# Block 0 of a fused attention forward and backward: hand-written PE and DVE lists in place of the unrolled ones

## The chip, the cores and the metric

One core of one Trainium2 chip. The metric is the device time of one execution in microseconds (us). TensorE is called PE, VectorE DVE, ScalarE ACT, GpSimd POOL, and SP is the engine that issues most DMAs.

## The reference: what is computed

A transformer block and the gradients of its input and its weights, for a sequence of 2048 rows of width 512 in bf16:

```
xn  = layernorm(x)
s   = attention(xn)            # 32 heads of 16 columns, softmax over 2048 keys, then @ wo
g   = silu(mlp(layernorm(xn))) # 512 -> 1792 -> 512, gelu
out = x + s * g
grads = vjp(out)(grad_out)     # for x, wqkv, wo, w1, b1, w2, b2
```

For each head the attention needs the scores q.k, their exponentials, and for the gradients the products dO.v, multiplied by the exponentials, in both orientations: with keys as rows (for what is summed over keys) and with queries as rows (for what is summed over queries).

## The kernel before, in words

The kernel has three stages: `phase_pre` (projections, the MLP forward; 0 to 208 us of the profile), `attention_core` (208 to 1980 us) and `phase3` (the remaining gradients). The change lies in `attention_core`.

**Blocks and steps.** Heads are taken in 16 pairs. A block is one pair and one quarter of the queries (512 of them), so there are 64 blocks; each has 16 steps, one for each 128 keys. Steps are numbered through, g = 0 to 1023; block 0 is g = 0 to 15. A step is made of units, each with a letter:

- `s` (PE, line 806): scores of 128 keys by 512 queries for both heads; two matmuls. `S` (ACT, line 834): the exponential, `et`.
- `d0`, `d1` (PE, line 828): the dO.v products of one head each, one matmul each, and `m0`, `m1` (DVE, line 845): their products with `et`, written to `gts`. Every second step SP turns a pair of steps of `gts` by a DMA transpose into `gk` (line 854).
- `a1` (PE, lines 865 and 868) and `a2` (line 878): sums over keys, from `et` and from `gts`, into one PSUM tile `X` that lasts a block. At the end of a block DVE copies X (`xs`), PE turns it (`XT`), DVE copies that (`xt`), and DVE and POOL make the rows' weights W1 and W2 from it (`sm`, lines 898 to 929).
- The q-major units belong to the block before: `t` (PE, line 818) and its exponential `T` (ACT, line 839), or, for 3 of the 16, a turned copy of `et`: `E` (PE transposes, line 790) and `eE` (DVE, line 795). Then `ze` and `zg` (PE, lines 938 and 946) sum over queries into `Z`, and `acc` (DVE, line 961) adds it up.

**The order.** PE, DVE and ACT run hand-written lists. `PE_ORDER` (line 691) and `DVE_ORDER` (line 699) hold one block's order, as unit and step; `unrolled` (line 976) repeats them for all blocks and drops what does not exist. A loop (line 1034) emits from the three lists in turn, as soon as what a unit needs has been emitted; on the chip each engine runs its list in order, and semaphores do the waiting. SP and POOL have no lists: a scheduler places their instructions.

In block 0 there is no block before it, so `t`, `T`, `ze`, `zg` and `acc` are dropped, and PE's list starts like this:

```
s:0 d1:0 s:1 d0:0 d1:1 s:2 d0:1 d1:2 a1:0 s:3 d0:2 d1:3 s:4 a1:1 a1:2 d0:3 a2:0 a2:1 a2:2 s:5 d1:4 d0:4 s:6 ...
```

and ends `... d1:13 s:14 d0:13 a1:11 d1:14 a2:11 s:15 d0:14 a1:12 a2:12 d1:15 E:11 s:16`. Here something else is put in, right behind each `s` from g = 2 on (line 1047): first the four pieces of `tail` that `phase_pre` left over (two sets of PE transposes of the last rows, line 311, and the two last projections `do_proj(14)` and `do_proj(15)`, line 324; each is followed by an ACT copy, lines 315 and 325, and DMAs), and from g = 6 to 15 two extra matmuls by `emit_warm` (line 1021), whose result nobody reads. That makes 20 of them.

**Buffers.** `s` and `t` share two PSUM tiles, so `s` of step g + 2 waits for `S` of step g. `d0` and `d1` have one PSUM bank each, so d0 of step g + 1 waits until m0 of step g has read it. `Z`, `ET`, `XT`, the `tail` pieces and the extra matmul (`warm`) take turns in one bank, the pool `ps_z`. There are 8 `et`, 4 `gts` (two steps each) and 6 `gk` tiles.

**PE's tiling.** `s` and `d` use 32 rows of the array each, so two matmuls of `s` and both of `d` can run side by side; `a1`, `a2`, `ze` and `zg` use all rows and 32 or 17 columns, so that four run side by side; `E` and the extra matmul use the whole array.

Of the kernel before, what the change touches and what calls it, by code (L numbers as in the profile page):

```python
# [690 lines left out]
PE_ORDER = """  # L691
# [7 lines left out]
DVE_ORDER = """  # L699
# [16 lines left out]
def attention_core(ctx, tc, opnds, ps_z, tail, NAT_s, NATQ_s, Oall, dQall, dKVT_out, ident_f32, ident_bf, npairs=16, nqc=4, turned=(0, 1, 2)):  # L716
# [124 lines left out]
    def emit_mult(g, hj):  # L841
        if g // 2 not in st_gts:
            st_gts[g // 2] = gtp.tile([128, 2, 2, 512], bf16, name="gts")
        gts = st_gts[g // 2]
        nc.vector.tensor_tensor(out=gts[:, g % 2, hj], in0=st_d.pop((g, hj))[:], in1=st_et[g][:, hj], op=ALU.mult)  # L845

    def emit_dmat(g):
        j, kb = divmod(g, 16)
        kc = kb // 4
        kbp = (kb // 2) % 2  # L850
        if kbp == 0:
            blk[j].setdefault("Gk", {})[kc] = gbp.tile([128, 2, 16, 128], bf16, name="gk")
        gk = blk[j]["Gk"][kc]
        nc.sync.dma_start_transpose(out=gk[:, kbp], in_=st_gts[g // 2][:].rearrange("k a h q -> k (a h q)"))
# [26 lines left out]
    def emit_xs(j):  # L881
        xs = xsp.tile([128, 512], f32, name="xs")
        nc.vector.tensor_copy(out=xs[:], in_=blk[j].pop("X")[:])
        blk[j]["xs"] = xs
# [8 lines left out]
    def emit_xt(j):  # L893
        xt = finp.tile([128, 4, 128], f32, name="xt")
        nc.vector.tensor_copy(out=xt[:], in_=blk[j].pop("XT")[:])
        blk[j]["xt"] = xt

    def emit_finish(j):
        p, qc = blocks[j]
        NQq = cur_op[p]["NATQq"]  # L900
        NQd = cur_op[p]["NATQd"]
        xt = blk[j].pop("xt")
        XTv = xt[:].rearrange("q b (r c) -> q b r c", r=4)
        W1 = wp.tile([128, 4, 2, 32], bf16, name="W1")
        W2 = wp.tile([128, 4, 2, 32], bf16, name="W2")
        nc.gpsimd.memset(W2[:, :, :, 0:16], 0.0)
        st0 = qc * 4
        nqs = NQq[:, st0:st0 + 4, :, 1:17]
        ndo = NQd[:, st0:st0 + 4, :, :]
        rL = finp.tile([128, 4, 2, 1], f32, name="rL")  # L910
        nc.vector.reciprocal(out=rL[:], in_=XTv[:, :, 2:4, 17:18])  # L911
        nc.gpsimd.tensor_tensor(out=W1[:, :, :, 0:16], in0=ndo, in1=rL[:].to_broadcast([128, 4, 2, 16]), op=ALU.mult)  # L912
        dl = finp.tile([128, 4, 2, 1], f32, name="dl")
        nc.vector.tensor_tensor(out=dl[:], in0=XTv[:, :, 2:4, 0:1], in1=rL[:], op=ALU.mult)
        ndr = finp.tile([128, 4, 2, 1], f32, name="ndr")
        nc.vector.scalar_tensor_tensor(out=ndr[:], in0=dl[:], scalar=-1.0, in1=rL[:], op0=ALU.mult, op1=ALU.mult)
        nc.gpsimd.tensor_tensor(out=W1[:, :, :, 16:32], in0=nqs, in1=ndr[:].to_broadcast([128, 4, 2, 16]), op=ALU.mult)
        nc.gpsimd.tensor_tensor(out=W2[:, :, :, 16:32], in0=nqs, in1=rL[:].to_broadcast([128, 4, 2, 16]), op=ALU.mult)
        Ov = Oall[:, st0:st0 + 4, p * 32:(p + 1) * 32].rearrange("q b (h c) -> q b h c", h=2)
        nc.gpsimd.tensor_tensor(out=Ov, in0=XTv[:, :, 0:2, 16:32], in1=rL[:].to_broadcast([128, 4, 2, 16]), op=ALU.mult)  # L920
        t1 = finp.tile([128, 4, 2, 16], f32, name="t1")
        nc.gpsimd.tensor_tensor(out=t1[:], in0=XTv[:, :, 0:2, 0:16], in1=dl[:].to_broadcast([128, 4, 2, 16]), op=ALU.mult)
        nc.gpsimd.tensor_tensor(out=t1[:], in0=XTv[:, :, 2:4, 1:17], in1=t1[:], op=ALU.subtract)
        rL4 = finp.tile([128, 4, 2, 1], f32, name="rL4")
        nc.gpsimd.tensor_scalar(out=rL4[:], in0=rL[:], scalar1=0.25, scalar2=None, op0=ALU.mult)
        dQv = dQall[:, st0:st0 + 4, p * 32:(p + 1) * 32].rearrange("q b (h c) -> q b h c", h=2)
        nc.gpsimd.tensor_tensor(out=dQv, in0=t1[:], in1=rL4[:].to_broadcast([128, 4, 2, 16]), op=ALU.mult)
        blk[j]["W1"] = W1
        blk[j]["W2"] = W2
# [43 lines left out]
    def turned_step(g):  # L973
        return g % 16 % 4 == 3 and g % 16 // 4 in turned

    def unrolled(order):
        items = [x.split(":") for x in order.split()]
        items = [(k, int(r)) for k, r in items]
        late = ("t", "T", "ze", "zg", "acc")
        return [(k, 16 * b + r) for b in range(-2, NB + 3) for k, r in items  # L980
                if (16 if k in late else 0) <= 16 * b + r < (NSTEP + 16 if k in late else NSTEP)]

    pe = unrolled(PE_ORDER)
    dve = unrolled(DVE_ORDER)
    act = []
    for g in range(NSTEP + 16):
        if g < NSTEP:
# [7 lines left out]
    issued = set()  # L995

    def needs(k, g):
        if k in ("s", "t"):
            i = place[("S" if k == "s" else "T", g)]
            return [act[i - 2]] if i >= 2 else []  # L1000
        if k in ("d0", "d1"):
            return [("m" + k[1], g - 1)] if g else []
        if k == "a1":
            return [("S", g)] + ([("xs", g - 1)] if g % 16 == 0 and g else [])
        if k == "a2":
            return [("m0", g), ("m1", g), ("a1", g - g % 16)]
        if k == "ze":
            e = ("eE", g - 16) if turned_step(g) else ("T", g)
            return [e, ("sm", g - g % 16 - 1)] + ([before[k, g]] if (k, g) in before else [])
        if k in ("E", "XT"):  # L1010
            return [("S", g) if k == "E" else ("xs", g)] + ([before[k, g]] if (k, g) in before else [])
        if k == "S":
            return [("s", g)]
        if k == "T":
            return [("t", g)]
        if k in ("m0", "m1"):
            return [("S", g), ("d" + k[1], g)]
        return {"acc": [("zg", g)], "xs": [("a1", g), ("a2", g)], "xt": [("XT", g)], "sm": [("xt", g)],
                "eE": [("E", g)], "zg": [("ze", g)]}[k]

    def emit_warm():

        w = ps_z.tile([128, 512], f32, name="warm", tag="z")
        nc.tensor.matmul(w[:], lhsT=cur_op[0]["KVT"][:, 0:128], rhs=cur_op[0]["KVT"][:, 0:512], start=True, stop=True)

    act_of = {"s": emit_s, "t": emit_t, "d0": lambda g: emit_d(g, 0), "d1": lambda g: emit_d(g, 1), "a1": emit_a1, "a2": emit_a2,
              "ze": emit_ze, "zg": emit_zg, "XT": lambda g: emit_XT(g // 16), "E": emit_E, "S": emit_exp_a, "T": emit_exp_b,
              "m0": lambda g: emit_mult(g, 0), "m1": lambda g: emit_mult(g, 1), "acc": emit_acc, "xs": lambda g: emit_xs(g // 16),
              "xt": lambda g: emit_xt(g // 16), "sm": lambda g: emit_finish(g // 16), "eE": emit_eE}
    ET_ = mybir.EngineType  # L1030
    with tc.manual_schedule(engines={ET_.PE, ET_.Activation, ET_.DVE}):
        lists = [act, dve, pe]
        at = [0, 0, 0]
        while any(a < len(l) for a, l in zip(at, lists)):
            moved = False
            for n, l in enumerate(lists):
                while at[n] < len(l) and all(x in issued for x in needs(*l[at[n]])):
                    k, g = l[at[n]]
                    act_of[k](g)
                    issued.add((k, g))  # L1040
                    at[n] += 1
                    moved = True
                    if k in ("m0", "m1") and g % 2 == 1 and ("m0", g) in issued and ("m1", g) in issued:
                        emit_dmat(g)
                    if k == "s":
                        j, kb = divmod(g, 16)
                        if tail and g >= 2:
                            tail.pop(0)()
                        elif 2 <= g < 16:
                            emit_warm()  # L1050
                            emit_warm()
                        p, qc = blocks[j]
                        if kb == 2 and qc == min(1, nqc - 1) and p + 1 < npairs:
                            load_pair(p + 1)
                        if g % 3 == 0 and load_q:
                            load_q.pop(0)()
                    if n == 2:
                        break
            assert moved, [l[a] for a, l in zip(at, lists) if a < len(l)]
# [116 lines left out]
```

## Time and profile before

| | us |
|---|---|
| median of 3 runs | 2370.25 (2368.81 to 2373.88) |
| the profiled execution | 2366.34 |
| its span, first to last instruction | 2364.3 |
| PE, ACT, DVE busy in the span | 2246.3, 2044.5, 2027.1 |
| first `s` of block 0 (step 0) | 208.15 |
| first `s` of block 1 (step 16) | 245.40 |
| last `s` (step 1023) | 1957.3 |

The profile's times count from the first instruction. A line of the timeline gives start, length, engine, source line, operation, tiles written and read, and how many were merged; in brackets stands the engine's idle time before it and what ended it. A line of the table by stretch gives, for each engine, the busy time and the number of instructions, then the TensorE clock that was granted (1.00 is full), the share of time in which the 16 DMA engines were busy, and what they moved. Consecutive `s` are 2.33 us apart in block 0 on average (37.25 us for 16 steps) and 1.70 us in the rest (1711.9 us for 1007 steps).

### The profile page before, as it was taken

To read this page: it belongs to the slowest core of one execution; us is meant where nothing else is said; L and a number is where in the kernel's file an instruction comes from. 1 tells how busy PE (TensorE), PEld (TensorE's weight loads), DVE (VectorE), ACT (ScalarE), POOL (GpSimd) and SP (SyncE) were. 2 spreads that over 40 slices of the span, in tenths; PEclk is the share of its full clock that TensorE was granted. 3 is DMA by queue.
4 is the path that set the end of the run, shared out by engine and by line. 5 is a ranking of instruction groups with operands and counts; after the bars stand their busy time and mean duration, and the time that the engine had idled before them with its cause. 6 is when DMAs were issued, how large, how long until landed. Compare 5 with 4: busy or idle time off the path is not lost.

```text
span 2364.3 us, 51036 instructions
## 1 busy us (share of the span) xinstructions
PE 2246.3 (95%) x20148; PEld 799.7 (34%) x20148; DVE 2027.1 (86%) x3600; ACT 2044.5 (86%) x2336; POOL 313.2 (13%) x753
## 2 busy tenths in 40 slices
PE   7897999999999999999999999999999998889698
PEld 3332333333333333333333333333333333334343
DVE  7566899999999999999999999999999996776164
ACT  6564899999999999999999999999999998783143
POOL 4221011111111111111111111111111112100000
PEclk9998999999999999999999999999999999999899
DMA  9877899999999999999999999999999997786961
GB/s 254 257 227 183 154 165 179 170 169 180 165 182 164 186 163 177 168 178 169 172 178 167 177 165 188 161 181 167 177 167 177 157 158 200 201 206 125 193 160 63
DMA packets 1349730, 415.56 MB, mean 176 GB/s; under 512 B 1272689, under 2 KB 1337586, under 8 KB 1349490
## 3 DMA queue, kind: packets, MB, share of 16 engines
q1 hardware_dynamic: 1346306, 403.66, 90.7%
q0 software_dynamic: 1600, 5.24, 0.6%
q8 instruction: 157, 2.57, 0.4%
q10 hardware_dynamic: 1584, 3.41, 0.4%
q14 instruction: 83, 0.68, 0.1%
HBM read 46.52 MB, written 49.03 MB: 40 GB/s over the span
## 4 chain that ended last, share of the span: by engine, by line
PE 74%; DVE 8%; issue 2%; ACT 2%; DMA 2%; SPq 1%; POOL 0%; ACTq 0%; DVEq 0%; POOLq 0%
PE d L828 12%; PE X L865 11%; PE s L806 11%; PE Z L946 9%; PE X L878 7%; PE Z L938 5%; DVE gts L845 5%; PE t L818 4%; PE ET L790 4%; PE XT L890 2%; PE ps_dw L574 1%; PE X L868 1%; PE ps_dy L629 1%; PE ps_dwkv L677 1%; PE ps_dhg L589 1%
## 5 line engine op out<-in xcount | busy, mean ns | idle before, releaser
L845 DVE TENSOR_TENSOR gts<-d,et 128x512 bf16<-128x512 f32 x2048 | 1321.7, 684 | 79.8 <-PE d L828 23.7
L834 ACT ACTIVATE et<-s 128x1024 bf16<-128x1024 f32 x1024 | 1043.6, 1044 | 15.1 <-PE s L806 12.9
L839 ACT ACTIVATE e<-t 128x1024 bf16<-128x1024 f32 x832 | 866.8, 1043 | 21.5 <-PE t L818 4.1
L828 PE MATMUL d<-QDT,KVT 32*128 32x512 bf16 x2048 | 759.7, 383 | 16.6 <-DVE gts L845 15.3
L806 PE MATMUL s<-QDT,KVT 32*128 32x512 bf16 x2048 | 398.0, 384 | 1.6 <-ACT et L834 1.1
L946 PE MATMUL Z<-gk,W 128*32 128x512 bf16 x2048 | 397.1, 384 | 0.0
L865 PE MATMUL X<-et,Lc 128*32 128x512 bf16 x2048 | 368.7, 388 | 0.0
L868 PE MATMUL X<-et,NAT 128*32 128x512 bf16 x2048 | 367.4, 387 | 0.0
L878 PE MATMUL X<-gts,NAT 128*17 128x512 bf16 x2048 | 329.4, 381 | 0.0
L818 PE MATMUL t<-KVT,QDT 32*128 32x512 bf16 x1664 | 323.2, 383 | 1.0 <-ACT e L839 1.0
L938 PE MATMUL Z<-e,W 128*32 128x512 bf16 x1664 | 321.5, 383 | 2.4 <-DVE ob L965 0.8
L828 PEld LDWEIGHTS <-KVT 32*128 32x128 bf16 x2048 | 173.7, 90 | 241.5 <-issue 241.4
L806 PEld LDWEIGHTS <-KVT 32*128 32x128 bf16 x2048 | 106.1, 91 | 244.0 <-issue 224.1
L912 POOL TENSOR_TENSOR W<-NATQd,rL 128x128 bf16<-128x128 bf16 x64 | 25.7, 402 | 1154.9 <-DVE rL L911 1154.9
L946 PEld LDWEIGHTS <-W 128*32 128x32 bf16 x2048 | 100.3, 95 | 172.1 <-issue 141.2
L818 PEld LDWEIGHTS <-QDT 32*128 32x128 bf16 x1664 | 92.3, 91 | 144.8 <-issue 139.9
L938 PEld LDWEIGHTS <-W 128*32 128x32 bf16 x2048 | 104.8, 94 | 105.1 <-issue 96.4
L865 PEld LDWEIGHTS <-Lc 128*32 128x32 bf16 x2048 | 83.3, 93 | 161.7 <-issue 161.6
L795 DVE COPY eE<-ET 128x1024 bf16<-128x1024 bf16 x192 | 130.0, 677 | 0.0
L790 PE MATMUL ET<-ident_bf,et 128*128 128x128 bf16 x1536 | 119.1, 220 | 0.2 <-DVE acc L961 0.2
L790 PEld LDWEIGHTS <-et 128*128 128x128 bf16 x1536 | 86.4, 98 | 43.7 <-issue 43.7
L878 PEld LDWEIGHTS <-NAT 128*17 128x17 bf16 x2048 | 79.2, 89 | 61.7 <-issue 44.8
(185 smaller groups left out, 2348.1 us busy)
## 6 DMA issues: line engine op xcount, KB each, us to landing
gk<-gts SPq DMA_TRANSPOSE x512, 4.5
H1T_s<-h1p SPq DMA_DIRECT2D x28, 256.0 KB, 4.1
HGT_s<-hgT SPq DMA_DIRECT2D x28, 256.0 KB, 4.4
h<-H1T_s SPq DMA_DIRECT2D x28, 256.0 KB, 3.3
NAT_s<-NS SPq DMA_DIRECT2D x4, 1056.0 KB, 7.0
do<-in_grad_out_dram SPq DMA_DIRECT2D x8, 512.0 KB, 4.8
GB_s<-gB POOLq DMA_DIRECT2D x16, 256.0 KB, 2.6
dKVT_s<-ob SPq DMA_DIRECT2D x16, 256.0 KB, 3.6
```

Source lines behind the costliest of these rows:

```text
L790: nc.tensor.transpose(ET[:, hj, m * 128:(m + 1) * 128], st_et[g - 3 + m][:, hj, 384:512], ident_bf[:])
L806: nc.tensor.matmul(s[:, hj, :], lhsT=op["KVT"][r, kb * 128:(kb + 1) * 128], rhs=op["QDT"][r, qc * 512:(qc + 1) * 512], start=True, stop=Tr ...
L818: nc.tensor.matmul(t[:, hj, :], lhsT=op["QDT"][r, q0:q0 + 128], rhs=op["KVT"][r, kc * 512:(kc + 1) * 512], start=True, stop=True, tile_pos ...
L828: nc.tensor.matmul(d[:], lhsT=op["KVT"][r, kb * 128:(kb + 1) * 128], rhs=op["QDT"][r, qc * 512:(qc + 1) * 512], start=True, stop=True, til ...
L834: nc.scalar.activation(out=et[:], in_=st_s.pop(g)[:], func=ACT.Exp)
L839: nc.scalar.activation(out=e[:], in_=st_t.pop(g)[:], func=ACT.Exp)
L845: nc.vector.tensor_tensor(out=gts[:, g % 2, hj], in0=st_d.pop((g, hj))[:], in1=st_et[g][:, hj], op=ALU.mult)
L865: nc.tensor.matmul(X[64 + 32 * hj:96 + 32 * hj, :], lhsT=Lc[:, :], rhs=et[:, hj, :], start=(kb == 0), stop=False, skip_group_check=True, t ...
L868: nc.tensor.matmul(X[32 * hj:32 * hj + 32, :], lhsT=NATt[:, kb, hj, 1:33], rhs=et[:, hj, :], start=(kb == 0), stop=(kb == 15), tile_positi ...
L878: nc.tensor.matmul(X[64 + 32 * hj:64 + 32 * hj + 17, :], lhsT=NATt[:, kb, hj, 0:17], rhs=gts[:, kb % 2, hj, :], start=False, stop=(kb == 1 ...
L938: nc.tensor.matmul(Z[32 * hj:32 * hj + 32, :], lhsT=blk[j]["W1"][:, qb, hj, :], rhs=e[:, hj, :], start=(qb == 0), stop=False, tile_positio ...
L946: nc.tensor.matmul(cur["Z"][32 * hj:32 * hj + 32, :], lhsT=blk[j]["W2"][:, qb, hj, :], rhs=grhs, start=False, stop=(qb == 3), tile_positio ...
```

## The change

Block 0 gets lists of its own, from `first_block`; what they hold is removed from the unrolled lists (`joined`). A new unit `W` takes the place of the code behind `s`: `W:1` to `W:4` run the four `tail` pieces, `W:0` and `W:5` to `W:13` one extra matmul each (`emit_warm`), so 10 in all.

```
-    pe = unrolled(PE_ORDER)
-    dve = unrolled(DVE_ORDER)
+    def first_block():
+
+        p = [("s", 0), ("s", 1), ("d1", 0), ("d0", 0)]
+        v = []
+        for g in range(14):
+            p += [("s", g + 2), ("W", g), ("d1", g + 1), ("d0", g + 1), ("a1", g)]
+            if g:
+                p.append(("a2", g - 1))
+            v += [("m1", g), ("m0", g)]
+            if g % 4 == 0 and g and g // 4 - 1 in turned:
+                p.append(("E", g - 1))
+                v.append(("eE", g - 1))
+        return p, v
+
+    def joined(first, rest):
+        done = set(first)
+        return first + [x for x in rest if x not in done]
+
+    p0, v0 = first_block()
+    pe = joined(p0, unrolled(PE_ORDER))
+    dve = joined(v0, unrolled(DVE_ORDER))
...
     def needs(k, g):
+        if k == "W":
+            return []
...
-    def emit_warm():
-
+    def emit_warm(g):
+
+        if tail and g:
+            tail.pop(0)()
+            return
         w = ps_z.tile([128, 512], f32, name="warm", tag="z")
         nc.tensor.matmul(w[:], lhsT=cur_op[0]["KVT"][:, 0:128], rhs=cur_op[0]["KVT"][:, 0:512], start=True, stop=True)
...
                     if k == "s":
                         j, kb = divmod(g, 16)
-                        if tail and g >= 2:
-                            tail.pop(0)()
-                        elif 2 <= g < 16:
-                            emit_warm()
-                            emit_warm()
```

PE's list then reads, through block 0 and into block 1,

```
s:0 s:1 d1:0 d0:0 | s:2 W:0 d1:1 d0:1 a1:0 | s:3 W:1 d1:2 d0:2 a1:1 a2:0 | s:4 W:2 d1:3 d0:3 a1:2 a2:1 | s:5 W:3 d1:4 d0:4 a1:3 a2:2
s:6 W:4 d1:5 d0:5 a1:4 a2:3 E:3 | s:7 W:5 d1:6 d0:6 a1:5 a2:4 | s:8 W:6 ... | s:10 W:8 d1:9 d0:9 a1:8 a2:7 E:7 | ...
s:14 W:12 d1:13 d0:13 a1:12 a2:11 E:11 | s:15 W:13 d1:14 d0:14 a1:13 a2:12 | d1:15 s:16 d0:15 d1:16 t:16 a1:14 a2:13 a2:14 s:17 ...
```

From `d1:15` on it is the old list. DVE's list has m1 and m0 of each step in turn, with `eE:3` behind m0:4 (before: behind m0:5), `eE:7` behind m0:8 (before: behind m1:10) and `eE:11` behind m0:12 (before: behind m1:15). On ACT the two copies of `tail`'s transposes stand behind S:3 and S:4 (before: behind S:1 and S:2), and the two of its projections behind S:5 and S:6 (before: behind S:3 and S:4). SP's order changes in a few places only: the transpose of pair 1's keys (KVT, line 761) moves ahead of the last transpose of pair 0's queries (line 336), and that of pair 1's queries (line 764) moves behind two more `gk` transposes.

## The prediction

> **What bounds the kernel now.** I read the spans and the clock first (span 2364.3 us, the profiled execution 2366.34, clock 0.988), then the table by stretch, to see where attention runs below its own pace:
>
> ```profile
> 208.15:245.40 37.25, 32.62 (x202) 9.39 (x202) 21.92 (x34) 18.61 (x21) 4.31 (x11) 0.91 0.93 182
> ...
> 219.49:245.40 25.91, 22.82 (x148) 6.65 (x148) 16.05 (x25) 11.64 (x12) 1.81 (x4) 1.00 1.00 187
> ...
> 300.00:600.00 300.00, 297.28 (x3070) 98.08 (x3072) 288.32 (x487) 296.84 (x321) 40.33 (x111) 1.00 1.01 173
> ```
>
> From block 1 on PE and ACT are both busy 99% of the time: nothing in the change touches that. In block 0 ACT is busy for 18.61 of 37.25 us and DVE for 21.92, and PE, busy for 32.62, sets the pace; from `s` of step 6 (219.49) to `s` of step 16 (245.40) a step takes 25.91 / 10 = 2.59 us. The PE timeline of the last steps shows on what:
>
> ```profile
> 240.24 0.39 PE L828 MATMUL d<-QDT,KVT 32*128 32x512 bf16 x1
> 240.25 0.39 PE L806 MATMUL s<-QDT,KVT 32*128 32x512 bf16 x2
> 240.57 0.82 PE L1024 MATMUL warm<-KVT 128*128 128x512 bf16 x2
> 241.32 0.38 PE L828 MATMUL d<-QDT,KVT 32*128 32x512 bf16 x1
> 241.63 0.39 PE L865 MATMUL X<-et,Lc 128*32 128x512 bf16 x2
> 241.64 0.39 PE L868 MATMUL X<-et,NAT 128*32 128x512 bf16 x2
> 241.97 0.39 PE L828 MATMUL d<-QDT,KVT 32*128 32x512 bf16 x1
> 242.28 0.39 PE L878 MATMUL X<-gts,NAT 128*17 128x512 bf16 x2
> 242.60 0.39 PE L806 MATMUL s<-QDT,KVT 32*128 32x512 bf16 x2
> 242.92 0.82 PE L1024 MATMUL warm<-KVT 128*128 128x512 bf16 x2
> ...
> 244.53 0.38 PE L828 MATMUL d<-QDT,KVT 32*128 32x512 bf16 x1
> 244.85 0.62 PE L790 MATMUL ET<-ident_bf,et 128*128 128x128 bf16 x8
> 245.40 0.39 PE L806 MATMUL s<-QDT,KVT 32*128 32x512 bf16 x2
> ```
>
> The starts give the prices. Each change of tiling costs 0.32 (s to warm, d to a1, a1 to d, a2 to s). From s over two warm matmuls to d it is 241.32 - 240.57 + 0.32 = 1.07; the two write one bank, so the second starts 0.43 behind the first. Two units of like tiling follow at 0.22 (a1 to a2). E takes 0.55 to the next s.
>
> **The change part by part.** (1) *Ten extra matmuls fewer*, 0.43 each on PE: 4.3 us. This is not added to what follows; the new chain, with one warm matmul, holds it.
>
> (2) *The new step on PE*: s, 0.32, W, 0.32, d1 and d0 side by side, 0.32, a1, 0.22, a2, 0.32, next s. That is 1.50 us. The loop with DVE is slower: from the traces, d's issue to m's start is 0.42 (241.32 to 241.74), m to m 0.60 with 0.69 to its end (two in 1.29), and d0 follows m0's end by 0.05. If d1 and d0 go at T, m0 ends at T + 0.42 + 1.29 = T + 1.71, the next d1 goes at T + 1.50, d0 at T + 1.76, then m1 at T + 1.92, m0 to T + 3.21, and both d at T + 3.26. So two steps take 3.26, and an ordinary step 1.63. ACT needs 1.02 of it; S is ready over a microsecond before m1 asks.
>
> (3) *A step with E*. E stands 0.32 + 0.22 behind d0, and 0.32 more for the change of tiling from a2, which no row shows: 0.22 (like tiling) to 0.32; I take 0.32. With d0 at 0, E goes at 0.86; eE starts 0.78 later (244.85 to 245.63) at 1.64 and ends at 2.32. DVE has nothing to do from -0.05 to 1.64, since eE now stands ahead of m1. s goes at 0.86 + 0.55 = 1.41; W, in the same bank as ET, waits for eE until 2.38 (0.65 lost), d1 for m1 until 2.98, d0 for m0 until 3.58. So 3.58 instead of 1.63. Queued behind W is all of PE; DVE waits for it. From one such step to the next it is 3.58 + 1.50 + 3.26 = 8.34 for four steps. Bounds of this wait: nothing (3 x 1.95 = 5.9 us less in all), or as much again for one of the three if bank and tiling cost more (2 us more).
>
> (4) *The start*. Up to d0:0 at 208.89 nothing changes. s:2 goes when S:0 ends (209.76 + 0.05 = 209.81, before: 210.54, behind d1:1, which waited for m1:0). Here the clock matters. In windows of 3.41 us:
>
> ```profile
> 202.80:206.21 3.41, 1.65 (x8) 0.56 (x6) 1.89 (x5) 1.75 (x4) 0.54 (x1) 1.00 0.21 80
> 206.21:209.62 3.41, 1.95 (x10) 0.52 (x11) 2.29 (x5) 3.25 (x6) 0.72 (x2) 1.00 0.46 144
> 209.62:213.04 3.42, 2.50 (x15) 0.67 (x14) 2.67 (x4) 2.37 (x4) 1.78 (x6) 0.50 1.02 243
> 213.04:216.45 3.41, 3.28 (x18) 1.06 (x14) 2.07 (x3) 1.71 (x3) 0.00 (x0) 0.50 1.00 177
> 216.45:219.86 3.41, 3.41 (x26) 0.96 (x26) 0.69 (x2) 1.78 (x3) 0.00 (x0) 1.00 0.20 40
> ...
> 247.17:250.58 3.41, 2.34 (x24) 0.66 (x23) 2.91 (x5) 3.41 (x5) 0.00 (x0) 1.00 0.81 152
> ```
>
> Two windows with PE busy 0.48 and 0.57 are followed by half a clock; a half window that is 0.73 busy is followed by another, one that is 0.96 busy by the full clock. 0.69 at the end did not bring it down. After the change the window from 209.62 is idle only until 209.81 and then issues at the half-clock pitch of 0.54 (211.09 to 211.63, the tail's transposes to d), each matmul lasting 0.6: some 0.94 busy. So I expect the full clock at 213.04. Then four pieces of tail follow, each held by an ACT copy of 0.59 that now stands behind an S: the first copy ends at 214.40 (S:3 from 212.87), the second set of transposes goes at 214.45 and d1:3 0.32 later at 214.77; s:5 goes at 215.91 and do_proj(14) 0.32 later at 216.23; d comes 0.98 behind a projection (218.51 to 219.49), so d:4 at 217.2; do_proj(15) waits for the copy behind S:5 until 218.38, and d0:5 goes at 219.36. With the half clock until 216.45, as before, d0:5 comes at 220.40.
>
> (5) *The end*. From d0:5 two periods (16.68), one step with E (3.58), then a1, a2, d1 and s of step 16 (0.32 + 0.22 + 0.32): 21.12, so 240.48 instead of 245.40, 4.92 earlier. Then t:16 is late, since d1:16 waits for m1:15: `s` of step 17 comes 2.24 behind that of step 16, where before S went on after 1.83 (245.88 to 247.71). That gives 0.41 back. From there ACT runs without a gap in both, so nothing more is won or lost: **4.5 us** in all (3.5 with the later clock).
>
> (6) *SP's order* costs nothing as far as I can see: DVE's wait for a gts tile comes eight steps after it was filled, while a transpose lands after 4.3 us, and pair 1 is not read before block 4.
>
> Sum: 2366.34 - 4.5 = 2361.8 for the profiled execution. The median lay 3.9 above that execution, so 2370.25 - 4.5 = **2365.7**.
>
> [...]
>
> **The rivals.**
>
> *The clock falls in block 0.* Ten matmuls that keep PE busy are gone, and W and d wait. By (2) and (3) PE idles about 1.0 us of each 8.34, in one piece of a window: at worst 0.70 busy. It decides below some 0.57 to 0.69, the rows above. Each half window does half of 3.41, so costs 1.7 us. Three eat the gain; all seven between 216.45 and 240.5 cost 11.9, and the time is 2370.25 - 4.5 + 11.9 = 2377.7, slower. For it: W's wait. Against it: at half clock PE would be busy without a pause, which brought the full clock back each time. Chance 0.08, of which most is a few windows (2366 to 2373).
>
> *The gain is given back in block 1*, because something that does not start earlier holds it, such as `gk` transposes (DMA share 1.0 in block 0 and after). Then 2370. Against it: they landed after 4.3 to 5.5 us throughout, and no row of PE or DVE waiting for a DMA in attention exceeds 1 us. Chance 0.07.
>
> *E costs little*: DVE and PE catch up the wait in (3). Then up to 5.9 more, 2360. In the trace nothing else is there for DVE to do at that point. Chance 0.1.
>
> That the lists do not come out as said can be excluded: the order of the built program has ten matmuls and ten weight loads less on PE, and the lists of the diff.
>
> **How the numbers follow.** My case has 0.75 and spans 2363 to 2368: the clock's two versions are 1.0 apart and executions differ by some 5 us (2368.8 to 2373.9), so that medians may be off by 2. 0.2% is 4.7 us, about what a measurement of this kernel can tell from no change, and the gain of 4.5 lies on that line: half of my case falls on each side. Range 2360 to 2372.5, which takes in cheap E steps and a few half windows. Faster 0.46, within 0.45, slower 0.09.
>
> **What would show it.** `s` of step 16 near 240.5 (241.5 with the later clock); ordinary steps 1.63 apart, those with E 3.6; DVE idle 1.7 ahead of each eE; W behind it waiting for eE; 1.00 from 213 on. Wrong if block 0 shows half windows behind 216, if s:16 comes after 243, or if the distance from step 16 to step 1023, now 1711.9, grows.

## The result, and the profile after

The changed kernel takes 2379.2 us (2378.45 to 2380.7, 6 runs) where the kernel before, beside it, takes 2371.59 (2368.81 to 2375.76, 6 runs): 1.0033 of it, 95% interval 1.0021 to 1.0045. The forecast was 2365.7. The profiled execution took 2379.14 us with a span of 2377.1, and the granted clock was 0.978 in the mean (before 0.988).

The table by stretch of the changed kernel, with the columns of the one shown for before; the long stretches are the whole of block 0 (first `s` to `s` of step 16), step 6 to step 16, and the later blocks; the others are windows of 3.41 us, at whose ends alone the granted clock changes in these traces:

```profile
208.97:251.25 42.28, 40.13 (x198) 9.39 (x198) 21.48 (x34) 18.71 (x21) 4.30 (x11) 0.59 0.77 153
221.28:251.25 29.97, 28.51 (x142) 6.68 (x141) 15.53 (x25) 10.76 (x11) 1.80 (x4) 0.60 0.75 142
300.00:600.00 300.00, 297.35 (x3066) 98.09 (x3060) 287.65 (x485) 296.57 (x321) 40.24 (x111) 1.00 1.00 172
...
209.98:213.39 3.41, 2.85 (x12) 0.52 (x10) 2.25 (x4) 2.44 (x3) 2.24 (x7) 0.50 1.02 254
213.39:216.80 3.41, 3.41 (x22) 1.12 (x20) 1.61 (x3) 1.98 (x3) 0.00 (x0) 0.50 0.99 181
216.80:220.22 3.42, 3.42 (x14) 0.66 (x12) 1.29 (x2) 2.04 (x3) 0.00 (x0) 0.50 0.31 60
220.22:223.63 3.41, 3.41 (x27) 1.02 (x27) 1.29 (x2) 2.13 (x3) 0.31 (x2) 1.00 0.73 135
223.63:227.04 3.41, 2.50 (x21) 0.81 (x18) 2.95 (x5) 1.02 (x1) 0.21 (x1) 1.00 1.01 192
227.04:230.46 3.42, 3.42 (x16) 0.58 (x14) 1.45 (x3) 1.46 (x2) 0.67 (x1) 0.50 0.73 171
230.46:233.87 3.41, 3.41 (x18) 0.60 (x19) 1.29 (x2) 1.61 (x2) 0.00 (x0) 0.50 1.08 207
...
261.18:264.59 3.41, 3.41 (x26) 0.72 (x24) 2.04 (x6) 2.05 (x2) 0.92 (x3) 0.50 0.24 46
264.59:268.01 3.42, 2.51 (x34) 1.00 (x27) 2.90 (x5) 3.29 (x4) 1.98 (x6) 1.00 0.82 153
```

Block 0 is 5.03 us longer, not 4.9 shorter, with ten matmuls less, and its mean clock is 0.59. The start has three half windows instead of two. Then comes one full window, one that is 0.73 busy (223.63), and from 227.04 the clock is at half for eleven windows, to 264.59, though PE is busy without a pause in five of them. The later blocks are as before.

What PE does in the window that lets the clock fall, and in the first half-clock steps (timeline; start, length, engine, line, operation, tiles, count, and in brackets the idle time before):

```profile
222.57 0.39 PE L828 MATMUL d<-QDT,KVT 32*128 32x512 bf16 x2
...
223.43 0.62 PE L790 MATMUL ET<-ident_bf,et 128*128 128x128 bf16 x8
...
223.98 0.39 PE L806 MATMUL s<-QDT,KVT 32*128 32x512 bf16 x2
...
224.09 0.69 DVE L795 COPY eE<-ET 128x1024 bf16<-128x1024 bf16 x1 [1.89 <-PE ET L790]
...
224.83 0.38 PE L1048 MATMUL warm<-KVT 128*128 128x512 bf16 x1 [0.46 <-DVE eE L795]
...
225.43 0.37 PE L828 MATMUL d<-QDT,KVT 32*128 32x512 bf16 x1 [0.22 <-DVE gts L845]
...
226.03 0.37 PE L828 MATMUL d<-QDT,KVT 32*128 32x512 bf16 x1 [0.23 <-DVE gts L845]
...
229.33 0.61 PE L806 MATMUL s<-QDT,KVT 32*128 32x512 bf16 x2
...
229.87 0.61 PE L1048 MATMUL warm<-KVT 128*128 128x512 bf16 x1
...
230.41 0.61 PE L828 MATMUL d<-QDT,KVT 32*128 32x512 bf16 x2
...
230.95 0.61 PE L865 MATMUL X<-et,Lc 128*32 128x512 bf16 x2
...
231.35 0.64 PE L878 MATMUL X<-gts,NAT 128*17 128x512 bf16 x2
...
231.92 0.61 PE L806 MATMUL s<-QDT,KVT 32*128 32x512 bf16 x2
```

The step with E is what the forecast said it would be: d0 to d0 3.46 us (222.57 to 226.03; forecast 3.58), the extra matmul waits for eE, d1 for m1 and d0 for m0, and DVE idles 1.89 us ahead of eE. What follows is not: a step at half clock is five groups of matmuls with PE never idle, 0.54 to 0.57 at each change of tiling and 0.40 between a1 and a2, in all 2.59 us (229.33 to 231.92) instead of the 1.63 forecast for an ordinary step.

**A measure.** PE's busy time does not tell these windows apart, so I counted for each window how long matmuls stream through the array (a matmul of 512 columns for 0.21 us at full clock, since four projections start 0.22 apart, from 208.00 to 208.66; for 0.43 at half, since they start 0.43 apart there, in before at 215.23, 215.66 and 216.09), each weighted with the share of the 128 rows that it uses: an `s` or `d` matmul counts a quarter, E, a1, a2 and the extra matmul count in full, those side by side on different columns once, and the fp32 transposes `XT` twice, since they start 0.11 apart (before, 251.11 to 251.33) where those of E start 0.06 apart (before, 244.92 to 245.25). I call this the *row share*. A record does not say when in its course the matmul streams; I take it from 0.1 us behind its start on, and another choice moves a window's share by some 0.02, rarely by more than 0.05. In the window from 223.63: E 0.34 (its start lies ahead of the window), s 0.11, extra 0.21, two d 0.11, a1 0.21, a2 0.21, the start of the next s 0.03, together 1.22 of 3.41 us, or 0.36. The half-clock step above: s 0.21, extra 0.43, d 0.21, a1 0.43, a2 0.43, or 1.71 of 2.59 us, 0.66. The windows of before had 0.38 to 0.72 in block 0 from 216.45 on, so the change's window lies below them, but only just. Some of the expectations below give shares that differ from this count by some 0.03.

**Theories.** *Rows*: the clock falls after a window with a low row share, and a fallen clock returns only after one with a far higher share. By this count it fell after 0.34 (before, from 206.21) and 0.36 (the changed kernel, from 223.63) and was kept after 0.38 (before, from 247.17); at half it stayed after 0.42 to 0.75 (the changed kernel, from 209.98 to 216.80 and from 227.04 to 261.18) and came back after 0.76 (before, from 213.04), 0.79 and 0.85 (the changed kernel, from 216.80 and 261.18). The lines between them, some 3/8 and some 3/4, are my estimate from these windows. The rivals: *busy time*, on which the forecast was built; *area* (rows times columns); and *order*, that the waits around E cost by themselves.

### The profile page after: what moved, and what is told of

Same layout as the page of the kernel before. It is cut to its first block, busy times and chain, and to the rows that moved or that the text cites. A ratio compares the mean times of both kernels' runs of the same rounds, so it can differ in the third digit from the quotient of the medians.

```text
span 2377.1 us, 51015 instructions
## 1 busy us (share of the span) xinstructions
PE 2259.4 (95%) x20138; PEld 801.0 (34%) x20138; DVE 2028.3 (85%) x3600; ACT 2045.1 (86%) x2336; POOL 312.9 (13%) x753
## 3 DMA queue, kind: packets, MB, share of 16 engines
q10 hardware_dynamic: 1584, 3.41, 0.4%
## 4 chain that ended last, share of the span: by engine, by line
PE 76%; DVE 7%; DMA 2%; ACT 2%; issue 2%; SPq 2%; POOL 0%; ACTq 0%; DVEq 0%; POOLq 0%
PE d L828 12%; PE X L865 11%; PE s L806 11%; PE Z L946 9%; PE X L878 7%; PE Z L938 5%; DVE gts L845 5%; PE t L818 5%; PE ET L790 5%; PE ps_dw L574 2%; PE XT L890 2%; PE X L868 1%; PE ps_dy L629 1%; PE ps_dwkv L677 1%; PE ps_dhg L589 1%
## 5 line engine op out<-in xcount | busy, mean ns | idle before, releaser
L878 PE MATMUL X<-gts,NAT 128*17 128x512 bf16 x2048 | 334.2, 385 | 0.0
```

Of the source, the lines that this page charges most:

```text
L878: nc.tensor.matmul(X[64 + 32 * hj:64 + 32 * hj + 17, :], lhsT=NATt[:, kb, hj, 0:17], rhs=gts[:, kb % 2, hj, :], start=False, stop=(kb == 1 ...
```

## The experiments

The kernel before ran beside each group of kernels on the same chip (medians 2368.5 to 2370.7); the ratios are to those. The *hand-over* is the passage from the last steps of block 0 to the first of block 1.

### What holds the clock: rows or columns

Both take the kernel before and change only the shape of its 20 extra matmuls, whose result nobody reads. `thin` gives them 32 rows, `narrow` 128 rows and 32 columns:

```
-        nc.tensor.matmul(w[:], lhsT=KVT[:, 0:128], rhs=KVT[:, 0:512], ...)
+        nc.tensor.matmul(w[:], lhsT=KVT[0:32, 0:128], rhs=KVT[0:32, 0:512], ..., tile_position=(0, 0))     # thin
+        nc.tensor.matmul(w[0:32, :], lhsT=KVT[:, 0:32], rhs=KVT[:, 0:512], ..., tile_position=(0, 0))      # narrow
```

> The kernel before, its 20 extra matmuls on 32 rows of the array instead of 128 (same 512 columns of input, same PE time). Row theory: the clock follows the share of PE's 128 rows through which data streams in a window of 3.41 us; it falls below about 3/8 and comes back from about 3/4. A step then streams 0.5 (s) + 0.5 (d) + 1 (a1) + 1 (a2) + 2 x 0.25 = 3.5 passes of 0.213 us in 2.5 us, 0.30: the clock falls to 0.50 in block 0 and stays there for 20 us or more; 2378 to 2385 us. Busy theory: the clock follows the time in which PE has anything to do, and its waits; this is as before, so 1.00 from 217 us on and 2370 us. Area theory (rows times columns): falls as well, like the row theory.

> The kernel before, its 20 extra matmuls on 128 rows and 32 columns of the array instead of 128 by 128 (same PE time). Row theory: the clock as before, 1.00 from 217 us on, 2370 us within 3 us. Area theory: the extra matmuls count a quarter, some 0.1 less in each window, so the clock falls in block 0 as in the changed kernel; 2378 us or more. Busy theory: as before, 2370.

`thin` took 2379.15 us (2377.78 to 2382.9), ratio 1.0042 (1.0027 to 1.0057); `narrow` 2369.17 (2365.08 to 2374.36), 0.9997 (0.9988 to 1.0007). The windows of `thin`:

```profile
215.93:219.34 3.41, 3.41 (x27) 0.93 (x26) 0.99 (x2) 1.63 (x3) 0.00 (x0) 1.00 0.25 49
219.34:222.76 3.42, 2.72 (x26) 0.95 (x22) 3.05 (x5) 2.57 (x4) 0.53 (x2) 1.00 0.98 186
222.76:226.17 3.41, 3.10 (x12) 0.58 (x11) 0.15 (x1) 1.57 (x2) 0.67 (x1) 0.50 0.93 209
226.17:229.58 3.41, 3.35 (x15) 0.58 (x13) 2.57 (x4) 1.25 (x2) 0.08 (x1) 0.50 0.98 187
229.58:233.00 3.42, 3.36 (x21) 0.72 (x19) 2.52 (x5) 1.02 (x1) 0.53 (x1) 0.50 1.05 195
```

and those of `narrow`:

```profile
222.26:225.68 3.42, 2.80 (x18) 0.65 (x17) 0.84 (x2) 2.05 (x2) 0.67 (x1) 1.00 0.97 209
225.68:229.09 3.41, 2.65 (x16) 0.77 (x14) 3.08 (x6) 1.31 (x2) 0.13 (x1) 1.00 0.99 194
```

In `thin` PE is busy 0.80 in the window from 219.34 (row share 0.37) and the clock falls; then PE is busy 0.91 to 0.98 (row shares 0.36, 0.57, 0.53) and it stays at half, to 256.89. In `narrow` PE is busy 0.82 and 0.78, with row shares of 0.50 and 0.38 but only 0.22 and 0.19 of the array's area, and the clock stays up. So busy time falls (before kept its clock after 0.69, from 247.17), and area falls for what brings the clock down (0.37 in `thin`'s window, 0.19 and 0.22 in those that kept it); rows remain. The shares 0.37 and 0.38 are too near each other to show it: what shows it is that the same number of matmuls held the clock on 128 rows and not on 32. Streaming counted without the weight for rows would rank the windows wrongly: 0.55 in `thin`'s, 0.45 in before's from 247.17. The old order, with extra matmuls that count a quarter, repeats the loss of the change.

### Which part of the change does it

`two_new`: the changed kernel with two extra matmuls in each W, in one sum. `turn_late`: the changed kernel with E (and eE) one step later, ahead of d, so that DVE has m1 and m0 to do while E runs. `one_old`: the kernel before with one extra matmul a step instead of two, in its old order.

```
+        for i in range(2):                                                         # two_new
+            nc.tensor.matmul(w[:], ..., start=(i == 0), stop=(i == 1))
...
+            turn = g % 4 == 1 and g > 1 and g // 4 - 1 in turned                   # turn_late
-            p += [("s", g + 2), ("W", g), ("d1", g + 1), ("d0", g + 1), ("a1", g)]
+            p += [("s", g + 2), ("W", g)] + ([("E", g - 2)] if turn else []) + [("d1", g + 1), ("d0", g + 1), ("a1", g)]
-            if g % 4 == 0 and g and g // 4 - 1 in turned:
-                p.append(("E", g - 1))
-                v.append(("eE", g - 1))
+            if turn:
+                v.append(("eE", g - 2))
...
                             emit_warm()                                            # one_old
-                            emit_warm()
```

> The changed kernel with two extra matmuls in each W that has one, written into one bank as one sum, so that they follow each other at 0.22 us: 20 instead of 10. Row theory: the window with the first E step, 0.38 in the changed kernel, gains 2 passes or more of 0.213 in 3.41, to 0.45 to 0.5: the clock stays at 1.00 in block 0; s of step 16 some 3 us earlier than before, 2367 to 2369 us. Wait theory: it was PE's waits in the E step (W for eE, d for m1 and m0, 0.9 us together) that let the clock fall; they are all still there, so it falls again, 2377 to 2382 us.

> The changed kernel with E of the turned units one step later and ahead of d instead of behind a2 (and eE behind that step's m0), so that neither W nor DVE waits for it; 10 extra matmuls, one in a step. Row theory: an E step streams 4 passes of 0.213 and 8 of 0.053 in some 2.1 us, 0.6, an ordinary one 0.52: the clock stays at 1.00 once it is back, s of step 16 about 6 us earlier than before, 2363 to 2366 us. Wait theory: stays at 1.00 too. Count theory (the 20 full-array extra matmuls of the kernel before are what keeps the clock up, ten do not): falls as in the changed kernel, 2377 us or more.

> The kernel before, old lists, with one extra matmul behind each s of steps 6 to 15 instead of two: half of the change alone. Row theory: an average step of 2.16 us streams 4 passes of 0.213, 0.39 of the rows, and windows in which PE waits less than 3/8: the clock falls in block 0 in most executions; then 2374 to 2382 us, and 2366 where it does not. Order theory (it is the new order with its wait for eE that let the clock fall): 1.00, and 4.3 us less than before, 2366.

`two_new` took 2372.7 us (2365.58 to 2378.17), 1.0007 (0.9996 to 1.0019), between what the two theories had said: its E windows have 0.45 and keep the clock, but in the profiled execution, the slowest of the ten, it falls at the hand-over (0.36), for six windows. `turn_late` took 2365.43 (2361.92 to 2381.44; eight of ten between 2361.9 and 2366.9), 0.9988 (0.9969 to 1.0008). `one_old` took 2363.62 (2360.82 to 2368.94), 0.9981 (0.9971 to 0.9992): I had expected its clock to fall, and it did not. Its steps became as much shorter as their matmuls became fewer (`s` of step 16 comes 32.95 us after the first, before 37.25), so that its windows in block 0 stayed at 0.41 or above; the hand-over, at 0.35, cost one half window.

The windows and then the timeline of `turn_late` around E:

```profile
223.67:227.08 3.41, 3.20 (x28) 1.10 (x28) 2.92 (x6) 2.05 (x2) 0.11 (x1) 1.00 1.01 192
...
240.73:244.15 3.42, 2.59 (x24) 0.69 (x23) 3.03 (x6) 2.36 (x3) 0.00 (x0) 1.00 1.12 181
244.15:247.56 3.41, 2.44 (x22) 1.01 (x20) 3.04 (x6) 3.41 (x5) 0.00 (x0) 1.00 1.06 192
```

```profile
224.13 0.61 PE L790 MATMUL ET<-ident_bf,et 128*128 128x128 bf16 x8
...
224.77 0.69 DVE L795 COPY eE<-ET 128x1024 bf16<-128x1024 bf16 x1 [0.49 <-PE ET L790]
...
225.53 0.39 PE L806 MATMUL s<-QDT,KVT 32*128 32x512 bf16 x2
...
225.85 0.39 PE L1048 MATMUL warm<-KVT 128*128 128x512 bf16 x1
...
226.71 0.37 PE L828 MATMUL d<-QDT,KVT 32*128 32x512 bf16 x1 [0.16 <-DVE gts L845]
```

DVE idles 0.49 us instead of 1.89 ahead of eE, the extra matmul waits for nothing, and the window has a row share of 0.47 instead of 0.36. Block 0 takes 32.30 us from the first `s` to that of step 16. The hand-over (0.43 and 0.38) is still weak, and two of the ten executions took 2377.8 and 2381.4, with a mean clock of 0.976 where the others have 0.981 to 0.986. The interval takes in 1 and ends below the changed kernel's: the rest of the change is not what loses time, the place of E is. Whether E's wait costs by itself or by way of the clock is the next question.

### The two weak places, mended with E left where it was put

`e_two` adds a second extra matmul in the three W behind an E, which wait anyhow; `e_two_hand` adds to that one extra matmul each in the two steps of the hand-over:

```
+        n = 2 if g in (5, 9, 13) else 1                                                       # e_two, e_two_hand
+        for i in range(n):
+            nc.tensor.matmul(w[:], ..., start=(i == 0), stop=(i == n - 1))
...
+        p += [("W", 14), ("d1", 15), ("s", 16), ("W", 15), ("d0", 15)]                        # e_two_hand
```

> The changed kernel with a second extra matmul in W:5, W:9 and W:13 only, the three that stand behind E. The second one lies beside the wait of d1 for m1 (0.22 there) and streams for 0.21 us on all rows. Row theory: the E steps are the weak place; the window around one had a row share of 0.38 in the changed kernel, and 0.21 more of 3.41 us makes it 0.44, above the 0.38 or 0.39 at which the clock fell or stayed. So the half clock in the middle of block 0 goes, at no price: s of step 16 near 242, the time near 2366. The hand-over (weakest window 0.36 to 0.38 in the two earlier kernels) can still let it fall in a part of the executions. Rival, busy time: PE is then busy 0.80 instead of 0.74 there, still more than windows of the old kernel that kept the clock at 0.69, so it makes no difference: 2379. Rival, ordinary steps are too thin as well (0.85 of 1.65 is 0.52, so I do not think so): falls all the same, 2376 to 2379.

> The changed kernel, its E where the change put it, with a second extra matmul in W:5, W:9 and W:13 and one extra matmul each in the two steps of the hand-over to block 1 (ahead of d1:15 and behind s:16), which had none. With the first part alone the profiled execution kept the full clock through all E steps (weakest window 0.43 in row share, before 0.38) and fell at the hand-over, at 0.38; two matmuls more there are 0.43 us of 3.41, so 0.50. Row theory: both weak places are mended, nothing else is left below 0.42, the clock stays up in nearly all executions and the time is what the arithmetic of the prediction gave, 2365 to 2368, with E unmoved. Rival, that E holds DVE and PE back is itself what costs: the time stays near that of the first part alone, 2373.

`e_two` took 2373.31 us (2369.83 to 2381.68), 1.0016 (1.0007 to 1.0026). In its profiled execution the E window is at 0.41 and keeps the clock, and the hand-over, at 0.35, loses it. `e_two_hand` took 2366.82 (2364.04 to 2377.47), 1.0005 (0.9992 to 1.0018). Its windows around the first E and the hand-over:

```profile
223.76:227.17 3.41, 2.72 (x20) 0.78 (x17) 3.07 (x5) 1.02 (x1) 0.09 (x1) 1.00 1.01 192
240.82:244.24 3.42, 2.73 (x17) 0.76 (x15) 2.92 (x6) 1.03 (x2) 0.00 (x0) 1.00 1.18 210
```

With five matmuls more no loss can be told: the interval takes in 1 and ends below the changed kernel's. In the profiled execution 1.00 holds from 220.34 on (these two windows 0.41 and 0.42), though E is where the change put it and the waits of 0.46 and 0.23 behind it are there; the second extra matmul fills the one of 0.22. So *order* falls as the cause of the loss; the clock is. The forecast gain isn't there either: the start has three half windows here too (d0:5 comes 13.72 us behind the first `s`, forecast 11.21), and from step 16 to step 1023 it takes 1713.8 us (forecast 1712.3). Three of the ten executions took 2370.9 to 2377.5. Only the slowest shows it in its mean clock (0.974, the others 0.982 to 0.986); what made the other two slow isn't known.

### Do the extra matmuls hold the clock up?

Three kernels without any extra matmul: the changed one (`after_none`), `turn_late` (`turn_late_none`) and the kernel before (`old_none`).

```
-        w = ps_z.tile([128, 512], f32, name="warm", tag="z")
-        nc.tensor.matmul(w[:], ...)
```

> The changed kernel without any extra matmul. Row theory: the window around an E step has even less (0.38 less 0.06), so the clock falls as in the changed kernel. At half clock a step with the extra matmul takes 2.59 us, five groups with four changes of tiling at 0.54 and one like tiling at 0.43; without it s and d follow each other in like tiling and the sum is 0.43 + 0.54 + 0.43 + 0.54 = 1.94, so a fallen clock costs 0.65 us less in each step. If the clock stays down as long, block 0 is up to 6 us shorter than in the changed kernel: 2372 to 2375. Rival, the extra matmuls, too few as they are, still hold the clock up in part: without them it is down longer, 2379 or more. Rival, busy time decides: 2379 to 2384, since PE is busy less.

> The changed kernel with E a step later and no extra matmul. Ordinary steps stay at about 1.65, since DVE sets them, so nothing is won by leaving the matmul out. Row theory: 0.64 of 1.65 is 0.39 in ordinary steps, on the line; with E 1.07 of 2.6 is 0.41; the hand-over is below. The clock falls in most executions: 2372 to 2380, against 2365.4 with the extra matmul. Rival, what matters is only that no engine waits for E: 2362 to 2366, as with the extra one.

> The kernel before, with its old lists and no extra matmul at all. With one instead of two the first s of block 0 to that of block 1 went from 37.25 to 32.95. Row theory: s, d, a1 and a2 alone stream 0.11 + 0.11 + 0.21 + 0.21 = 0.64 us of full rows a step, which at 1.6 us a step is 0.40, on the line between falling and staying; so the clock falls in block 0 in a large part of the executions, those are 5 to 12 us longer than the others, and the median is 2365 to 2374. Rival, the extras only cost time now that the rest keeps PE going: up to 4 us less than with one, 2359 to 2362, in all executions.

`after_none` took 2371.19 us (2368.55 to 2376.41), 1.0014 (1.0004 to 1.0024), just below the expected range; `turn_late_none` 2366.76 (2362.3 to 2376.25), 0.9991 (0.9979 to 1.0003); `old_none` 2368.99 (2366.26 to 2374.84), 0.9991 (0.9982 to 0.9999). I had expected `turn_late_none` to fall in most executions; three of eleven lie above 2373. A half-clock step of `after_none`:

```profile
227.51 0.61 PE L806 MATMUL s<-QDT,KVT 32*128 32x512 bf16 x2
227.52 0.61 PE L828 MATMUL d<-QDT,KVT 32*128 32x512 bf16 x2
...
228.06 0.61 PE L865 MATMUL X<-et,Lc 128*32 128x512 bf16 x2
...
228.46 0.63 PE L878 MATMUL X<-gts,NAT 128*17 128x512 bf16 x2
...
229.03 0.61 PE L806 MATMUL s<-QDT,KVT 32*128 32x512 bf16 x2
```

It takes 1.52 us, where I had expected 1.94: without the extra matmul between them `s` and `d` run side by side. So the one extra matmul of the change costs up to 2.59 - 1.52 = 1.07 us in a half-clock step. Most gain less, since waits fill a part: from `s` of step 8 to that of step 16 `after_none` takes 19.50 us (225.65 to 245.15) and the changed kernel 24.38 (226.87 to 251.25), 0.61 a step. At full clock it isn't free either, as I had expected it to be: from `s` of step 9 to that of step 13 `turn_late_none` takes 6.47 us (226.86 to 233.33) and `turn_late` 7.50 (227.55 to 235.05), 0.26 a step. In `after_none` too the clock falls at the first E (row share 0.30) and stays down, for seven windows, but block 0 takes 37.5 us (207.64 to 245.15) instead of 42.3. In the changed kernel one extra matmul a step is too little to hold the clock and enough to make its fall dear.

### The start, and versions that beat both

`before_fill`, `turn_late_fill`, `turn_late_fill_hand` and `one_old_fill` put twelve full matmuls into the pause ahead of block 0, between `do_proj(12)` and `do_proj(13)`; `turn_late_fill_hand` has the line of `e_two_hand` as well.

```
+        fill = psA.tile([128, 512], f32, name="fill", tag="mm")
+        for i in range(12):
+            nc.tensor.matmul(fill[:], lhsT=w2_sb[:, 0, 0:128], rhs=w2_sb[:, 1, :], start=(i == 0), stop=(i == 11))
```

> The kernel before with 12 matmuls that nobody needs, 128 by 128 by 512, in one sum, put where PE waits 2.7 to 2.9 us for an ACT copy ahead of the last projection (just ahead of the first s). Row theory: the window that let the clock fall there, 0.34 to 0.35 of the rows, gains up to 0.7: no half clock at 210 to 217, which costs block 0's first steps some 2 to 3 us; 2367 to 2369 us and 1.00 from 200 us on. If the wait of PE itself or the switch to 32-row matmuls lets the clock fall, the half windows stay and the time is that of the kernel before or up to 1 us more.

> The new lists with E one step later and ahead of d, ten extra matmuls, and the 12 matmuls in PE's wait ahead of the first s. Row theory: 1.00 all through block 0; s of step 16 some 3 us earlier against the first s than without the 12, 2361 to 2363 us; in the few executions in which the window at the hand-over to block 1 (0.36 to 0.42 of the rows) falls under 3/8, 2375 or more. Rival: the 12 matmuls delay the last projection and with it everything; then 2365 or more.

> As turn_late_fill, with two more extra matmuls at the hand-over to block 1, ahead of d1 of step 15 and behind s of step 16, where PE waits 0.52 and 0.21 us for DVE. Row theory: the weakest window of block 0 rises from 0.36 to 0.42 by 0.06 to 0.12, so no execution falls to the half clock: all within 2360 to 2366 us. If the executions near 2378 to 2381 of turn_late have another cause, they come back here.

> The old lists with one extra matmul a step, and twelve full-array matmuls at the start. Row theory: as with one alone (2363.6), less what the half clock at the start costs where the filler keeps it away (nothing to 3 us): 2361 to 2364. No rival differs by more; it is there to see whether a version beats both kernels.

| | us | ratio (95%) |
|---|---|---|
| `before_fill` | 2367.31 (2364.75 to 2369.17) | 0.9994 (0.9985 to 1.0003) |
| `turn_late_fill` | 2363.73 (2359.05 to 2365.95) | 0.9980 (0.9970 to 0.9989) |
| `turn_late_fill_hand` | 2363.27 (2360.36 to 2365.31) | 0.9978 (0.9969 to 0.9988) |
| `one_old_fill` | 2366.79 (2364.33 to 2368.53) | 0.9984 (0.9975 to 0.9992) |

In the profiled execution of `turn_late_fill` the half clock at the start is gone; in the other three a window of 0.23 to 0.31 in row share behind the filler still lets the clock fall, for one or two windows. In that of `before_fill` it falls again at the hand-over (0.36, for four windows), where the kernel before had kept it at 0.38. The filler's worth can't be told from nothing, since the intervals with and without it overlap. What beats both kernels, by some 0.2%, is the new order with E one step later and the filler, or the old order with one extra matmul a step instead of two, which needs nothing else.

## Why the prediction was wrong

The miss, along the profiled execution (forecast for it 2361.8, measured 2379.14): the start 2.4 us (first `s` to d0:5 13.60 instead of 11.21), d0:5 to `s` of step 16 7.6 (28.68 instead of 21.12), step 16 to step 1023 4.1 (1716.4 instead of 1712.3), and 3.3 outside the attention (0.8 ahead of the first `s`, 2.5 behind the last), where the change does nothing and executions differ.

**(1) to (3): right in their numbers.** Ordinary steps, forecast 1.63, are 3.31 us for two in `turn_late` (`s` at 227.55, 229.06 and 230.86); the E step 3.58, measured 3.46; DVE's idle time 1.7, measured 1.89; the waits are the three that it named. That DVE sets the ordinary step is not the whole, since the step is 0.26 shorter without its extra matmul. The price of the extra matmuls in (1) holds as well: ten fewer in the old order took 4.3 us off block 0 (37.25 to 32.95 in `one_old`). With the clock held, `e_two_hand` goes from d0:5 at 222.58 to `s` of step 16 at 243.73 in 21.15 us; the sum of step (5) was 21.12.

**(4): failed.** "A half window that is 0.73 busy is followed by another, one that is 0.96 busy by the full clock" was read as a rule. The window from 209.98 was 0.84 busy, the next was busy without a pause, and both were followed by half windows. By rows they have 0.42 and 0.65; the one that brought the full clock, from 216.80, has 0.79, as before's from 213.04 had 0.76. The table that the forecast shows spoke against busy time already: its window from 202.80, 0.48 busy, was followed by a full one, and the next, 0.57 busy, by a half one. By rows they have 0.46 and 0.34.

**(5) and the first rival: the mechanism was named, its conditions were wrong, and that is the step that failed.** Step (5) added up 21.12 us as if the full clock held, and 28.68 were measured. The rival "decides below some 0.57 to 0.69" of PE busy; PE was busy 0.73 when the clock fell. I had even worked out that the worst window would be "at worst 0.70 busy", and took the old windows of that kind as cover. But the change took out matmuls on all rows and left those on 32 rows, which count a quarter: PE as busy as in windows that kept the clock (0.73; before 0.69, from 247.17), with a lower row share (0.36; before 0.38). The argument against it, that "at half clock PE would be busy without a pause, which brought the full clock back each time", is the second error: in eleven half windows PE was busy 0.75 to 1.00, and only the last, at 0.85 by rows, ended it. The rival's price fits in sum (11.9 forecast; 7.6 + 4.1 = 11.7 in block 0 and block 1) and not in its parts: it was to be seven windows at 1.7 and was eleven at about 1.06 (24.2 us at half clock in block 0 cost 7.6, the 13.3 in block 1 cost 4.1), since DVE and the waits would have filled a part of the time anyhow. Of the 4.1 some 1.5 stand in `e_two_hand` too, whose clock held (1713.8 against 1712.3). That the sum fits is luck; on the two errors the rival had been given a chance of 0.08.

**The waits of PE**, which the first rival had on its side with "W's wait", are not the whole. The clock dropped with no pause above 0.46 us in the window, but `turn_late` keeps the waits for d's banks (0.16 at 226.71) and `e_two_hand` keeps two of the three (0.46 and 0.23), and both keep the clock. Nor did a window without a pause bring it back: those from 213.39 and 227.04, busy throughout, did not.

**(6) and the other rivals.** SP's order shows no cost: in the changed kernel the one wait of PE or DVE for a DMA in the attention is 0.2 us, of a weight load for `gk`. Some gain is given back in block 1, more than the 0.41 of step (5): from step 16 to step 1023 `e_two_hand` takes 1713.8 and `turn_late` 1714.1 us, before 1711.9. E did not come cheap (3.46).

**What stays open.** Of all windows from 200 to 300 us in the sixteen traces, at full clock, the 7 below 0.32 were all followed by half a clock and the 338 above 0.42 by none; between them 18 fell and 20 stayed. All but one that fell had 0.37 or less, and all that stayed had 0.375 or more, so that one line between 0.37 and 0.375 misplaces 1 of 383 windows (1 or 2, wherever from 0 to 0.16 us behind its start a matmul is taken to stream); the best line misplaces 17 by busy time, 24 by area, and 8 by streaming without the weight for rows. At half clock the 34 below 0.62 all stayed down, the 10 from 0.79 on all came back, and between them 24 stayed and 15 came back. The best line, near 0.75, misplaces 7 of 83, by area 11, and no line by busy time is better than to let none come back (25); so what brings the clock back is less sure than what brings it down, and rows and area are not told apart there. The lines were found on the same windows that they divide, windows at 0.36 and 0.38 differ by less than a single matmul, some matmul records are missing from a trace, and no run measured such lines by themselves: they are estimates from these windows.

## What to carry to other kernels

Before matmuls are taken out, count for the weakest window of the clock what streams over all rows of the array, not PE's busy time: in `thin` extra matmuls on a quarter of the rows kept PE busy for 0.80 of the window from 219.34, and the clock fell to 0.50. A wait is then best moved, as E was, to where another engine has work (DVE idled 0.49 us ahead of eE instead of 1.89); a filler matmul belongs into the window that is weak, and one spread over all steps cost most here with the clock fallen (0.61 us a step, 0.26 at full clock). If a state is lost at one level and regained at another, as here (lost after 0.36 in row share, regained after 0.85), ask of a rival not only whether it starts but whether it can end.

## What the runs showed of the hardware

- In this kernel 20 extra matmuls on 32 rows by 128 columns let the granted clock fall to 0.50 in block 0 (`thin`, after the window from 219.34; 2379.15 us); the same number on 128 rows by 32 columns held it at 1.00 there (`narrow`, from 215.44 on; 2369.17 us).
- What lost the clock and what brought it back lie far apart in row share: in the sixteen traces, from 200 to 300 us, all but one of the 25 windows after which it fell had 0.37 or less, and it came back after none of the 34 below 0.62 and after all 10 from 0.79 on. The changed kernel streamed 0.47 to 0.75 at half clock for ten windows and stayed there, and came back after an eleventh of 0.85; in five of the eleven PE was never idle.
- Here fewer extra matmuls were both better and worse: in the order of the change none, one, two a step gave 1.0014, 1.0033 and 1.0007 of the time before, and five well placed on top of one a step 1.0005.
